# Which queue brings the first blocks of x and w1, and where TensorE's first run over w1 stands among x's turns

## The chip, the core and the metric

The kernel runs on one NeuronCore of a Trainium2 chip. The core has a matrix engine (TensorE, PE in the profile; its weight loads are PEld), VectorE (DVE), ScalarE (ACT), GpSimd (POOL) and a queue engine (SyncE, SP). Sixteen DMA engines move data between DRAM and the core's SBUF; transfers are issued here by SP and by ScalarE. Matmul results go to eight PSUM banks of 512 float32 columns. The metric is the device time of one execution in microseconds (us), taken as the median of several; smaller is better.

## The reference

The forward pass of a two-layer block with a tanh-approximated gelu, and its gradients. All inputs and outputs are bfloat16: x and grad_out are 2048 x 448, w1 is 448 x 1792, w2 is 1792 x 448.

```python
def _fwd_reference(x, w1, b1, w2, b2):
    h = jnp.einsum("bsd,df->bsf", x, w1) + b1
    h = _gelu(h)
    return jnp.einsum("bsf,fd->bsd", h, w2) + b2
# outputs: the result, and its gradients to x, w1, b1, w2, b2 for grad_out
```

## The kernel before

Rows of x (S = 2048) are worked in four blocks of 512; the 1792 hidden columns are 14 tiles of 128, taken as seven pairs. For each block and pair TensorE computes u = w1^T x^T (hidden columns on partitions, rows of x on the free axis), the other engines make gelu(u) and its derivative, and TensorE computes q = w2 grad_out^T and the products that use them. At the end come the gradients of w1 and w2, each a long sum over all rows. 448 is three times 128 plus 64, so a product over it is cut in halves of 64 contraction rows, and two halves run on TensorE at the same time in its upper and lower rows; in the profile one matmul "64*128 64x512" is one of two that run together, a pair.

Nothing is scheduled by a planner. Five tables of names, one for each engine (`PE_ORDER`, `ACT_ORDER`, `DVE_ORDER`, `SP_ORDER`, and a short list for GpSimd), give the order in which each engine's instructions are issued, and waits between engines follow from what each step reads and writes. An engine works through its list in order, so a step that waits holds back all behind it on that engine. DMAs signal their landing on eight semaphore slots (DMAHW0 to DMAHW7) in turn, in the order in which they are put into the program; the DMA that takes a slot for the second time waits on its queue until the first holder has landed.

The change touches the first ten microseconds. The names there are:

- On SP and ScalarE: `xr01`, `xr12`, `xr24` load rows 0 to 127, 128 to 255 and 256 to 511 of x (x's tiles 0, 1, and 2 and 3; function `LXN`, line 558 in the profile as for all plain loads) into `TR`. `L0` to `L4` load five parts of w1's first 384 rows into `w1f`; `L1` is in two pieces. `Z0` to `Z2` load its last rows, the left-over of 448 beyond 3 x 128, into `gh_nat`. `b1` is the first bias. `K0`, `K1` and so on load w2. `L1a` waits for the identity matrix.
- On VectorE: `ident` builds the identity (line 613 is its last step); `X0.0`, `X1.0`, `X2.1`, `X3.1` copy turned tiles of x from PSUM to SBUF (`XC`, line 633), and `b1T` copies the turned bias. ScalarE copies the other halves, after its table load (line 765).
- On TensorE: `W6` is six matmuls on constants, 128 x 512, that only wake the engine (`wake`, line 389). `X0` to `X3` turn x's four tiles against the identity (`XT`; eight matmuls of 64 columns each). `F6` is six pairs on constants, 128 columns wide (`fill`). `S0` is the first run over w1: pair 0, columns of x's tiles 0 and 1, all contraction rows at once in four banks (`U` with d = 3, `uq_run`). It issues second(0), second(1), then first(0) to first(3), then second(2); first(3) and second(2) read w1's left-over rows. `B` turns the bias. `T1` is pair 0 over x's tiles 2 and 3, one tile at a time. `u1.1`, `h1.2`, `u1.2`, `u2.1`, `u3.1` are further runs over w1: `u2.1` needs its third part (`L2`), `u3.1` the fourth (`L3`). `p0.0` is the first product that needs a gelu.
- All runs of halves are issued in the function `run`, so their matmuls share line 242. In lines 440, 442, 444 and 455 the first values of u get their bias.

The matmuls of S0 go to banks 4 to 7; the constants of W6 and F6 go to `qb`, that is banks 6 and 7, and are overwritten.

Of the kernel before, what the change touches and what calls it, by code (L numbers as in the profile page):

```python
# [88 lines left out]


PE_ORDER = """
W6 X0 X1 F6 X2 X3 S0 B T1 u1.1 h1.2 u1.2 u2.1 u3.1 u2.2 u3.2 p0.0 p0.1 p0.2 p0.3 p1.0 p1.1 p1.2 u4.1 u5.1 u4.2
u5.2 p1.3 p2.0 p2.1 p2.2 p2.3 u6.1 p3.0 u6.2 p3.1 p3.2 p3.3 p4.0 p4.1 u7.1 p4.2 u7.2 p4.3 p5.0 p5.1 p5.2 p5.3 u8.1
p6.0 u8.2 q0.1 p6.1 q0.2 u9.1 p6.2 u9.2 q1.1 p6.3 q1.2 u10.1 o1.0.0.6.1 u10.2 q2.1 o1.1.0.6.1 u11.1 q2.2 u11.2
o1.0.0.6.2 o1.1.0.6.2 q3.1 u12.1 q3.2 u12.2 o1.0.6.10.1 q4.1 o1.1.6.10.1 u13.1 q4.2 u13.2 o1.0.6.10.2 q5.1 o1.1.6.10.2
# [11 lines left out]
x3.1.6.10.1 x3.0.6.10.2 x3.1.6.10.2 x3.0.10.14.1 x3.1.10.14.1 x3.0.10.14.2 x3.1.10.14.2  # L107
"""
ACT_ORDER = """
xr12 L0 Z0 table X0.1 X1.1 X2.0 X3.0 k0A k0B c0A1 s0 g0 s1 g1 c2B t0 s2 g2 g3 s3 c5B g4 t1 t2 c6B g5 g6 s4 s5 g7 c8A c8B g8 c9A c9B  # L110
g9 c10A c10B t3 t4 g10 s6 c11A c11B s7 g11 t5 c12A c12B g12 s8 t6 c13A c13B g13 s9 t7 s10 t8 c14A c14B t9 g14 s11 s12
c15A c15B t10 g15 c16A c16B s13 t11 g16 c17A c17B s14 t12 g17 c18A c18B s15 g18 vx0.2 c19A c19B t13 t14 g19 s16 c20A
c20B s17 g20 t15 s18 t16 s19 c21A c21B t17 g21 c22A c22B s20 t18 g22 c23A c23B g23 s21 t19 s22 t20 s23 c24A c24B t21
# [12 lines left out]
vx3.3  # L126
"""
SP_ORDER = """
xr01 xr24 b1 L1a L1b Z1 L2 L3 K0 K1 L4 Z2 K2 K3 X1 R F b2 Y0 J0 J1 J2 Y1 I0 E J3 I1 So0.1 So0.0 X2 H0 H1 H2 H3 H4 H5 H6 H7 H8 H9
T0 T1 H10 T2 H11 T3 H12 T4 H13 T5 So1.0 So1.1 T6 T7 H14 T8 Y2 H15 T9 X3 H16 T10 H17 Sx0.0 Sx0.1 T11 H18 H19 T12 H20  # L130
T13 T14 T15 So2.0 Y3 H21 So2.1 T16 H22 H23 T17 T18 T19 H24 Sx1.0 T20 Sx1.1 H25 T21 H26 Nx H27 T22 T23 Sx2.0 Sx2.1 T24
T25 T26 So3.0 So3.1 Ng T27 Sx3.0 Sx3.1
# [28 lines left out]
def make_plan(tc, ctx, x, w1, b1, w2, b2, grad_out, out_0, out_1, out_2, out_3, out_4, out_5):  # L161
    nc = tc.nc
    P = 128
    _, S, D = x.shape
    F = w1.shape[1]
    NS, NF, SB = S // P, F // P, 512
# [7 lines left out]
    g2 = grad_out.rearrange("b s d -> (b s) d")  # L174
# [11 lines left out]
    w1_sb = w1f[:, 0:4 * F].rearrange("p (k f) -> p k f", k=4)  # L186
# [6 lines left out]
    xT = [sb.tile([P, 4, EDGE + SB], BF16, name=f"xT{i}") for i in range(2)]  # L193
# [23 lines left out]
    def bk_(i):  # L217
        return BK[i][:, :] if i < 6 else qb[:, i - 6, :]
# [8 lines left out]
    def run(slots, idle=False):  # L227


        first = slots[0]  # L230
        prev = [tail_of.get((first[i][0], 1 - i), (0, None, False)) for i in (0, 1)]
        prev = max([t for i, t in enumerate(prev) if t[2] or not first[i][4]], default=(0, None), key=lambda t: t[0])
        n_run[0] += 1
        word = None
        if prev[0] > seen[0]:
            word = nc.gpsimd.nop()  # L236
            tc.add_manual_dep(word.ins, prev[1].ins.name, DEP, reason="the run has ended")
            seen[0] = prev[0]
        for two in slots:
            for i, (b, n, l, r, st, sp) in enumerate(two):  # L240
                at, n = n if isinstance(n, tuple) else (0, n)
                m = nc.tensor.matmul(bk_(b)[:, at:at + n], lhsT=l, rhs=r, start=st, stop=sp, skip_group_check=True)  # L242
                if word is not None:
                    tc.add_manual_dep(m.ins, word.ins.name, DEP, reason="the halves change banks")
                    word = None
        for i in (0, 1):
            tail_of[slots[-1][i][0], i] = (n_run[0], m, idle)

    def uq_run(w, t, banks, pair, d, c0=0, c1=SB, at=0):

        ft = (2 * (pair % NPB), 2 * (pair % NPB) + 1)

        def plain(i, k, low, st, sp, banks=banks):
            rows = slice(0, 64) if low else slice(64, 128)
            cols = slice(ft[i] * P, (ft[i] + 1) * P)
            return (banks[i], (at, c1 - c0), w[rows, k, cols] if k < 3 else w1z[rows, cols], t[rows, k, EDGE + c0:EDGE + c1], st, sp)

        if w is w1_sb and pair < NPB and d < 3:
            if d == 1:
                run([(plain(1, k, True, k + at == 0, False), plain(0, k, False, k + at == 0, False)) for k in (0, 1, 2, 3)])
            else:
                run([(plain(0, k, True, False, k == 2), plain(1, (0, 1, 3)[k], False, False, k == 2)) for k in (0, 1, 2)])
            return

        if d == 3:
            one_, two = banks[:2], banks[2:]

            def first(k):
                return [plain(1, k, True, k == 0, k == 3, one_), plain(0, k, False, k == 0, k == 3, one_)]

            def second(k):
                return [plain(0, k, True, k == 0, k == 2, two), plain(1, (0, 1, 3)[k], False, k == 0, k == 2, two)]

            run([second(0), second(1)])
            run([first(k) for k in range(4)])
            run([second(2)])
            return  # L280
# [48 lines left out]
    def part_w1(p):  # L329
        return ("w1", W1_PART[p % NPB])  # L330

    def U(p, d, hf=None, by_tile=False):
        b = p // NPB
        if hf is None:
            bk, hs, c, tag = u_banks(p), (0, 1), (0, SB), ""
            vs = [bank(("u", p, 0), bk[0]), bank(("u", p, 1), bk[1])]
        else:
            bk, hs, c, tag = ((4, 5), (0, 1))[hf], (hf,), (256 * hf, 256 * hf + 256), f"h{hf}"
            vs = [bank(("u", p, 0, hf), bk[0]), bank(("u", p, 1, hf), bk[1])]
            if d == 3:  # L340
                bk = bk + (6, 7)
                vs += [bank(("ux", p, 0), 6), bank(("ux", p, 1), 7)]
        rd = [part_w1(p)] + [("xT", b, h) for h in hs] + ([("w1z", REST[p])] if b == 0 else ["w1r"])
        if d == 2 and b > 0:
            rd += [("xe", b), "w1f"]
        def fn():
            for a in range(c[0], c[1], P) if by_tile else (c[0],):
                uq_run(w1_sb, xT[b % 2], bk, p, d, a, a + P if by_tile else c[1], a - c[0])

        pe(f"u{p}.{d}{tag}", fn, rd, vs,  # L350
           ("s512" if hf is None else "s256", 2 + d), (bk, d))

    def Q(p, d):
# [169 lines left out]
    for i, t in enumerate([t for t in SP_ORDER.split() if t[0] == "S"]):  # L523
        b, half = t[2:].split(".")
# [166 lines left out]
    def num(t):  # L691
        return [int(i) for i in t.split(".")]

    for t in PE_ORDER.split():
        k, a = t[0], t[1:]
        if k == "w":
            wake(int(a), P)
        elif k == "W":
            wake(int(a))
        elif k == "X":  # L700
            XT(int(a))
        elif k == "f":
            fill(int(a), (3, 2), 2 * P)
        elif k == "F":
            fill(int(a), (6, 7), 2 * P)
        elif k == "B":
            pe("b1u", lambda: nc.tensor.matmul(bk_(5)[:, 256:272], lhsT=b1n[0:64, :], rhs=ident[0:64, 0:16], start=True, stop=True,  # L707
                                               skip_group_check=True), ["b1n", "b1z", "ident"], [val(("b1u",), ("bank5b",))], ("s16", 1), (None, 0))
        elif k == "d":
            DM(*num(a))  # L710
        elif k == "h":
            hf, d = num(a)
            U(0, d, hf)
        elif k == "S":
            U(0, 3, int(a))
        elif k == "T":
            U(0, 1, int(a), True)
        elif k in "uqp":
            {"u": U, "q": Q, "p": OP}[k](*num(a))
        else:  # L720
            b, half, f0, f1, d = num(a)
            UN(k, b, half, list(range(f0, f1)), d)
# [52 lines left out]
    for t in SP_ORDER.split():  # L775
        k, a = t[0], t[1:]
# [57 lines left out]
    for ft in range(NF):  # L834
        bk = next_bank()
# [8 lines left out]
        fn = (lambda dst=dst, src=src: nc.scalar.mul(out=dst, in_=src, mul=-0.5)) if eng == "ACT" else \  # L844
# [3 lines left out]
        c = ft // 4  # L848
# [37 lines left out]
    for ft in range(NF):  # L886
        halves = [(0, D)] if ft < NF - 1 else [(0, D - P), (D - P, D)]
        for (d0, d1) in halves:
            bk = next_bank()
# [8 lines left out]
            fn = (lambda dst=dst, src=src: nc.scalar.copy(out=dst, in_=src)) if eng == "ACT" else \  # L898
# [38 lines left out]
```

## Time and profile before

| What | Value |
|---|---|
| median of 3 runs | 263.88 us (263.86 to 264.1) |
| span of the profiled execution, first to last instruction | 262.2 us |
| TensorE busy | 258.8 us, 99% |
| VectorE busy | 199.5 us, 76% |
| ScalarE busy | 127.6 us, 49% |
| chain of waits that ended last | PE 99% |
| mean rate of all DMA | 178 GB/s |

The device time of a run contains what lies before the first and after the last instruction; the span does not. For the profiled execution only the span is told. A row of the timeline gives the start in us from the span's start, the length, the engine, the line, the operation, what is written and read, shapes and the count; neighbours of one form are merged. In brackets stands the idle time before it and what ended that. A matmul's length is longer than the distance to the next, since they are pipelined; the pace is read from the starts.

### The profile page before, as it was taken

Reading aid. Unit: us, or ns where it says so; the run is one execution under the profiler, and the core shown is the slowest. Engines: PE = TensorE matmul, PEld = TensorE weight load, DVE = VectorE, ACT = ScalarE, POOL = GpSimd, SP = SyncE. Lnnn points to the kernel's source line nnn. Section 1 sums busy time; section 2 is a strip of 40 time slices with the busy share of each in tenths; the row PEclk is TensorE's granted clock in tenths of the full one; section 3 lists DMA queues with packets and bytes.
Section 4 is the critical chain, followed back from the end, with each engine's and each line's share of the span. In section 5 each row is a group of like instructions: output and inputs, shape, how many; then the busy total and the mean of one; then the engine's idle time right before and its main releaser. Section 6 shows DMA issues by size and latency. Waiting matters only on the chain.

```text
span 262.2 us, 5415 instructions
## 1 busy us (share of the span) xinstructions
PE 258.8 (99%) x2217; PEld 149.5 (57%) x2217; DVE 199.5 (76%) x287; ACT 127.6 (49%) x166; POOL 14.2 (5%) x11
## 2 busy tenths in 40 slices
PE   8999999999999999999999999999999999999995
PEld 5444455555555666666666677765555555555554
DVE  5999398999989989999997995249999999310000
ACT  5899569936898956875896310011121111000001
POOL 1000000000000000000000000000000392400000
PEclk9999999999999999999999999999999999999999
DMA  6999989999999892972487824974899999975221
GB/s 201 292 249 171 197 127 197 258 341 212 244 180 220 236 228 43 195 203 43 107 203 257 216 42 63 262 211 106 162 217 136 184 213 171 235 152 158 72 70 35
DMA packets 120633, 46.61 MB, mean 178 GB/s; under 512 B 96686, under 2 KB 120479, under 8 KB 120608
## 3 DMA queue, kind: packets, MB, share of 16 engines
q1 hardware_dynamic: 119920, 45.82, 78.0%
q10 hardware_dynamic: 688, 0.44, 0.6%
q8 instruction: 17, 0.28, 0.4%
q14 instruction: 8, 0.07, 0.1%
HBM read 8.20 MB, written 14.28 MB: 86 GB/s over the span
## 4 chain that ended last, share of the span: by engine, by line
PE 99%; ACT 0%; issue 0%
PE bank L242 48%; PE qb L242 18%; PE bank L839 16%; PE bank L893 16%; PE qb L389 1%; ACT w_sb L898 0%; PE bank L707 0%
## 5 line engine op out<-in xcount | busy, mean ns | idle before, releaser
L242 PEld LDWEIGHTS <-HG 64*128 64x128 bf16 x896 | 55.7, 94 | 32.2 <-POOLq L236 2.1
L242 PE MATMUL qb<-gT,w2Tf 64*128 64x512 bf16 x392 | 52.9, 376 | 0.0
L242 PE MATMUL bank<-w_sb,HG 64*128 64x448 bf16 x448 | 48.4, 349 | 0.0
L242 PE MATMUL bank<-xT,w1f 64*128 64x512 bf16 (+2 forms) x361 | 47.3, 368 | 0.0
L242 PE MATMUL bank<-w1T_sb,HG 64*128 64x448 bf16 x448 | 47.2, 349 | 0.0
L515 DVE SCALAR_TENSOR_TENSOR HG<-TR,qb 128x1024 bf16<-128x1024 bf16 x28 | 34.1, 1217 | 12.6 <-PE qb L242 12.6
L893 PE MATMUL bank<-w2Tf,HG 128*128 128x448 bf16 (+2 forms) x240 | 42.6, 340 | 0.0
L839 PE MATMUL bank<-w1f,gh_nat 128*128 128x448 bf16 x224 | 42.5, 352 | 0.0
L893 PEld LDWEIGHTS <-HG 128*128 128x128 bf16 x240 | 22.9, 98 | 19.8
L839 PEld LDWEIGHTS <-gh_nat 128*128 128x128 bf16 x224 | 21.8, 98 | 20.6 <-issue 0.4
L242 PEld LDWEIGHTS <-w2Tf 64*128 64x128 bf16 x392 | 24.1, 94 | 16.6 <-POOLq L236 0.3
L500 ACT ACTIVATE TR<-TR 128x1024 bf16<-128x1024 bf16 x28 | 29.2, 1052 | 6.6 <-DVE TR L490 6.6
L242 PEld LDWEIGHTS <-w1f 64*128 64x128 bf16 x388 | 22.0, 94 | 17.3 <-POOLq L236 0.7
L862 DVE TENSOR_TENSOR w1T_sb<-w1T_sb,gh_nat 128x1792 f32<-128x1792 f32 x14 | 28.4, 2025 | 0.5
L844 ACT ACTIVATE TR<-bank 128x448 bf16<-128x448 f32 x14 | 7.6, 543 | 34.9 <-PE bank L839 34.9
L899 DVE CAST w_sb<-bank 128x448 bf16<-128x448 f32 x6 | 3.7, 624 | 25.9 <-PE bank L893 25.9
L898 ACT CAST w_sb<-bank 128x448 bf16<-128x448 f32 (+2 forms) x9 | 4.4, 490 | 37.7 <-PE bank L893 37.7
L868 POOL PARTITION_ALL_REDUCE w1T_sb<-w1T_sb x1 | 10.6, 10570 | 206.0 <-DVE w1T_sb L866 206.0
L475 ACT ACTIVATE TR<-gh_nat 128x1024 bf16<-128x1024 bf16 x15 | 15.7, 1052 | 11.5 <-DVE TR L510 11.5
L505 DVE TENSOR_SCALAR TR<-TR 128x2048 bf16<-128x2048 bf16 x28 | 19.2, 688 | 1.9 <-ACT TR L500 1.9
L495 DVE TENSOR_TENSOR TR<-TR,HG 128x1024 bf16<-128x1024 bf16 x28 | 19.2, 684 | 0.0
L510 DVE TENSOR_TENSOR TR<-TR 128x1024 bf16<-128x1024 bf16 x28 | 19.0, 686 | 0.1
(54 smaller groups left out, 190.6 us busy)
## 6 DMA issues: line engine op xcount, KB each, us to landing
hT_dram<-HG SPq DMA_DIRECT2D x28, 256.0 KB, 3.2
out_dram<-st SPq DMA_DIRECT2D x16, 224.0 KB, 3.3
w1f<-in_x_dram SPq DMA_DIRECT2D x2, 896.0 KB, 6.0
w2Tf<-in_grad_out_dram SPq DMA_DIRECT2D x1, 1792.0 KB
out_dram<-w_sb SPq DMA_DIRECT2D x2, 448.0 KB, 2.8
out_dram<-xT SPq DMA_DIRECT2D x2, 384.0 KB, 3.4
w_sb<-in_w_dram SPq DMA_DIRECT2D x1, 672.0 KB
w1f<-in_w_dram SPq DMA_DIRECT2D x1, 576.0 KB
```

The source lines that it names most:

```text
L242: m = nc.tensor.matmul(bk_(b)[:, at:at + n], lhsT=l, rhs=r, start=st, stop=sp, skip_group_check=True)
L475: pl.op("ACT", f"s{p}", lambda: nc.scalar.activation(out=TR[p % NTR][:, 1], in_=ubuf(p), func=ACT.Square, scale=sc), [("ub", p)], [v], ("a ...
L495: pl.op("DVE", f"R{p}", lambda: nc.vector.tensor_tensor(out=t[:, 1], in0=t[:, 1], in1=hblk(p), op=ALU.mult), [("r", p), ("h", p)], [val((" ...
L500: pl.op("ACT", f"t{p}", lambda: nc.scalar.activation(out=t[:, 0], in_=t[:, 0], func=ACT.Tanh), [("y", p)], [val(("t", p), ("TR0", p % NTR) ...
L505: pl.op("DVE", f"m{p}", lambda: nc.vector.tensor_scalar(out=t[:], in0=t[:], scalar1=1.0, scalar2=None, op0=ALU.subtract), [("t", p), ("r2" ...
L510: pl.op("DVE", f"n{p}", lambda: nc.vector.tensor_tensor(out=t[:, 0], in0=t[:, 0], in1=t[:, 1], op=ALU.mult), [("m0", p), ("m1", p)], [val( ...
L515: pl.op("DVE", f"G{p}", lambda: nc.vector.scalar_tensor_tensor(out=ghblk(p), in0=t[:, 0], scalar=2.0, in1=qb[:, :, :], op0=ALU.subtract, o ...
L839: nc.tensor.matmul(bk_(bk)[:, 0:D], lhsT=gh_nat[:, st // 4, ft, st % 4, :], rhs=x_nat[:, st, :], start=(st == 0), stop=(st == NS - 1))
L844: fn = (lambda dst=dst, src=src: nc.scalar.mul(out=dst, in_=src, mul=-0.5)) if eng == "ACT" else \
L862: nc.vector.tensor_tensor(out=hs3, in0=a, in1=gh_nat[:, st // 4, :, st % 4, :], op=ALU.add)
L868: pl.op("POOL", "gb1", lambda: nc.gpsimd.partition_all_reduce(gb1_w, hsum, channels=P, reduce_op=bass_isa.ReduceOp.add), ["hsc"], ["gb1"], ...
L893: nc.tensor.matmul(bk_(bk)[:, 0:d1 - d0], lhsT=h_nat[ft][:, st, :], rhs=g_nat[:, st, d0:d1], start=(st == 0), stop=(st == NS - 1))
```

## The change

ScalarE's queue no longer loads x's tile 1: its first two DMAs are now w1's first part and the left-over rows. SP loads tile 1 as its second DMA, ahead of tiles 2 and 3. On TensorE there is one waking matmul less (W5), two fill pairs now stand between X0 and X1 and five behind X1 (seven for six), and S0 is cut into four parts: S0.1 (second(0), second(1)) and S0.2 (first(0), first(1)) come ahead of X2 and X3, S0.3 (first(2), first(3)) and S0.4 (second(2)) behind them.

```diff
 PE_ORDER = """
-W6 X0 X1 F6 X2 X3 S0 B T1 u1.1 h1.2 u1.2 u2.1 u3.1 u2.2 u3.2 p0.0 ...
+W5 X0 F2 X1 F5 S0.1 S0.2 X2 X3 S0.3 S0.4 B T1 u1.1 h1.2 u1.2 u2.1 u3.1 u2.2 u3.2 p0.0 ...
...
 ACT_ORDER = """
-xr12 L0 Z0 table X0.1 X1.1 X2.0 X3.0 k0A k0B ...
+L0 Z0 table X0.1 X1.1 X2.0 X3.0 k0A k0B ...
...
 SP_ORDER = """
-xr01 xr24 b1 L1a L1b Z1 L2 L3 K0 K1 ...
+xr01 xr12 xr24 b1 L1a L1b Z1 L2 L3 K0 K1 ...
...
-            run([second(0), second(1)])
-            run([first(k) for k in range(4)])
-            run([second(2)])
+            run([[second(0), second(1)], [first(0), first(1)], [first(2), first(3)], [second(2)]][part - 1])
             return
```

On TensorE, at the place where the first run over w1 begins, stood before, behind X3's turns (`TR` is x, `st` the identity, `w1f` w1, `qb` and `bank` are PSUM, `xT` the turned x):

```order
99 L242 LDWEIGHTS TR_80
100 L242 MATMUL bank_92<-st_81,TR_80 128x64
101 L242 LDWEIGHTS w1f [waits DMAHW2_49]
102 L242 MATMUL qb<-xT_68,w1f 128x256
103 L242 LDWEIGHTS w1f
104 L242 MATMUL qb<-xT_68,w1f 128x256
```

Now the run's first matmul stands behind the fill, and waits for VectorE's and ScalarE's copies too; X2 stands behind the run's first eight matmuls, and the other six (four, then two) behind X3:

```order
69 L242 LDWEIGHTS const-bfloat16-1.0
70 L242 MATMUL qb<-const-bfloat16-1.0 128x128
71 L242 LDWEIGHTS w1f [waits DVE_49,DMAHW0_49]
72 L242 MATMUL qb<-xT_68,w1f 128x256 [waits Activation_49]
```

```order
85 L242 LDWEIGHTS w1f
86 L242 MATMUL bank_93<-xT_68,w1f 128x256
87 L242 LDWEIGHTS TR_80 [waits DMAHW4_49]
88 L242 MATMUL bank_89<-st_81,TR_80 128x64
```

Here X2 and X3 no longer wait for banks to be copied out, as the run between has waited for that already.

On SP, the first DMAs before:

```order
1 L558 DMA TR_80<-in_x_dram 128x448
2 L558 DMA TR_80<-in_x_dram 128x2x448
3 L558 DMA b1n<-in_b_dram 14x128 [waits Pool_49]
4 L558 DMA w1f<-in_w_dram 128x2x256 [waits DVE_49]
5 L558 DMA w1f<-in_w_dram 128x256
6 L558 DMA gh_nat<-in_w_dram 128x512 [waits DMAHW0_49]
7 L558 DMA w1f<-in_w_dram 128x3x256 [waits DMAHW1_49]
```

and now:

```order
1 L556 DMA TR_80<-in_x_dram 128x448 x2
2 L556 DMA TR_80<-in_x_dram 128x2x448
3 L556 DMA b1n<-in_b_dram 14x128 [waits Pool_49]
4 L556 DMA w1f<-in_w_dram 128x2x256 [waits DVE_49]
5 L556 DMA w1f<-in_w_dram 128x256
6 L556 DMA gh_nat<-in_w_dram 128x512 [waits DMAHW0_49]
7 L556 DMA w1f<-in_w_dram 128x3x256 [waits DMAHW1_49]
```

Row 1 now holds two loads, tiles 0 and 1. Row 6, `Z1`, still waits for slot 0; that slot was held by x's tile 1 on ScalarE's queue (X1 waited for it) and is now held by w1's first part (S0.1 waits for it).

More of the change, by code (lines that the diff above doesn't have):

```diff
@@ L91 @@
 PE_ORDER = """
-W6 X0 X1 F6 X2 X3 S0 B T1 u1.1 h1.2 u1.2 u2.1 u3.1 u2.2 u3.2 p0.0 p0.1 p0.2 p0.3 p1.0 p1.1 p1.2 u4.1 u5.1 u4.2
+W5 X0 F2 X1 F5 S0.1 S0.2 X2 X3 S0.3 S0.4 B T1 u1.1 h1.2 u1.2 u2.1 u3.1 u2.2 u3.2 p0.0 p0.1 p0.2 p0.3 p1.0 p1.1 p1.2 u4.1 u5.1 u4.2
 u5.2 p1.3 p2.0 p2.1 p2.2 p2.3 u6.1 p3.0 u6.2 p3.1 p3.2 p3.3 p4.0 p4.1 u7.1 p4.2 u7.2 p4.3 p5.0 p5.1 p5.2 p5.3 u8.1
@@ L109 @@
 ACT_ORDER = """
-xr12 L0 Z0 table X0.1 X1.1 X2.0 X3.0 k0A k0B c0A1 s0 g0 s1 g1 c2B t0 s2 g2 g3 s3 c5B g4 t1 t2 c6B g5 g6 s4 s5 g7 c8A c8B g8 c9A c9B
+L0 Z0 table X0.1 X1.1 X2.0 X3.0 k0A k0B c0A1 s0 g0 s1 g1 c2B t0 s2 g2 g3 s3 c5B g4 t1 t2 c6B g5 g6 s4 s5 g7 c8A c8B g8 c9A c9B
 g9 c10A c10B t3 t4 g10 s6 c11A c11B s7 g11 t5 c12A c12B g12 s8 t6 c13A c13B g13 s9 t7 s10 t8 c14A c14B t9 g14 s11 s12
@@ L128 @@
 SP_ORDER = """
-xr01 xr24 b1 L1a L1b Z1 L2 L3 K0 K1 L4 Z2 K2 K3 X1 R F b2 Y0 J0 J1 J2 Y1 I0 E J3 I1 So0.1 So0.0 X2 H0 H1 H2 H3 H4 H5 H6 H7 H8 H9
+xr01 xr12 xr24 b1 L1a L1b Z1 L2 L3 K0 K1 L4 Z2 K2 K3 X1 R F b2 Y0 J0 J1 J2 Y1 I0 E J3 I1 So0.1 So0.0 X2 H0 H1 H2 H3 H4 H5 H6 H7 H8 H9
 T0 T1 H10 T2 H11 T3 H12 T4 H13 T5 So1.0 So1.1 T6 T7 H14 T8 Y2 H15 T9 X3 H16 T10 H17 Sx0.0 Sx0.1 T11 H18 H19 T12 H20
@@ L247, in run, with uq_run @@
             tail_of[slots[-1][i][0], i] = (n_run[0], m, idle)
-    def uq_run(w, t, banks, pair, d, c0=0, c1=SB, at=0):
+    def uq_run(w, t, banks, pair, d, c0=0, c1=SB, at=0, part=0):
         ft = (2 * (pair % NPB), 2 * (pair % NPB) + 1)
@@ L330, in part_w1, with U @@
         return ("w1", W1_PART[p % NPB])
-    def U(p, d, hf=None, by_tile=False):
+    def U(p, d, hf=None, by_tile=False, part=0):
         b = p // NPB
@@ L347, in fn @@
             for a in range(c[0], c[1], P) if by_tile else (c[0],):
-                uq_run(w1_sb, xT[b % 2], bk, p, d, a, a + P if by_tile else c[1], a - c[0])
-        pe(f"u{p}.{d}{tag}", fn, rd, vs,
+                uq_run(w1_sb, xT[b % 2], bk, p, d, a, a + P if by_tile else c[1], a - c[0], part)
+        pe(f"u{p}.{d}{tag}.{part}", fn, rd, vs,
            ("s512" if hf is None else "s256", 2 + d), (bk, d))
@@ L714, in make_plan @@
         elif k == "S":
-            U(0, 3, int(a))
+            hf, part = num(a)
+            U(0, 3, hf, part=part)
         elif k == "T":
```

## Prediction

> **What bounds the kernel now.** I read the page first (busy shares, chain of waits), then a table of windows to see where TensorE (PE) ever stops, then the timeline of the first 10 us by engine, then the DMA issues of that stretch with their time to landing.
>
> ```profile
> PE 258.8 (99%) x2217; PEld 149.5 (57%) x2217; DVE 199.5 (76%) x287; ACT 127.6 (49%) x166; POOL 14.2 (5%) x11
> PE 99%; ACT 0%; issue 0%
> 9.01:258.00 248.99, 248.99 (x2089) 143.56 (x2090) 193.96 (x269) 121.96 (x155) 13.44 (x2) 1.00 0.80 179
> ```
>
> The second row is the chain of waits: PE carries it. The third is the windows view: from 9.01 to 258 us PE is busy 248.99 of 248.99 us. The work there is the same in both kernels, so the change reaches the end only by moving the moment at which this unbroken stretch begins, and that is u3.1, the first run over w1's fourth part. The start, in PE's timeline (start, length, group, count), with some rows taken from narrow windows so that groups are cut where I need them:
>
> ```profile
> 2.85 0.63 PE L389 MATMUL qb<-const-bfloat16-1.0 128*128 128x512 bf16 x1
> 3.41 0.61 PE L242 MATMUL bank<-st,TR 64*128 64x64 bf16 x16
> ...
> 3.62 0.40 PE L242 MATMUL bank<-st,TR 64*128 64x64 bf16 x8
> 3.83 0.83 PE L242 MATMUL qb<-const-bfloat16-1.0 64*128 64x128 bf16 x12
> 4.45 0.51 PE L242 MATMUL bank<-st,TR 64*128 64x64 bf16 x16
> 4.80 0.38 PE L242 MATMUL qb<-xT,w1f 64*128 64x256 bf16 x4
> 5.02 0.49 PE L242 MATMUL bank<-xT,w1f 64*128 64x256 bf16 x6
> ...
> 5.56 0.35 PE L242 MATMUL bank<-xT,w1f 64*128 64x128 bf16 x6
> ...
> 5.89 0.34 PE L242 MATMUL bank<-xT,w1f 64*128 64x128 bf16 x6
> ...
> 8.38 0.40 PE L242 MATMUL qb<-xT,w1f 64*128 64x512 bf16 x2
> 8.59 0.40 PE L242 MATMUL qb<-xT,gh_nat 64*128 64x512 bf16 x2
> 9.00 0.11 PEld L242 LDWEIGHTS <-w1f 64*128 64x128 bf16 x4 [0.51 <-DMA w1f<-in_w_dram]
> ```
>
> In order: the last of the six waking matmuls (2.85); X0 and X1, the turns of x's tiles 0 and 1 (3.41, 3.62); the fill F6 (3.83); X2 and X3 (4.45); S0 (4.80); T1's two tiles (5.56 and 5.89). The runs behind follow one another until u2.1's last pair at 8.59, a pair every 0.21, so PE is free at 8.80 and u3.1, at 9.01, has waited 0.2 us for a load of w1. There are two speeds: six fill pairs of 128 columns take 0.62 us (3.83 to 4.45), 0.10 each; two S0 pairs of 256 columns take 0.22 (4.80 to 5.02), 0.11 each. PE runs at half rate until about 4.65, although the granted clock reads 1.00 throughout.
>
> The other rows that count are VectorE's, which make the identity and copy x's turns to SBUF (ScalarE copies the other half, faster), and the loads:
>
> ```profile
> 2.63 0.25 DVE L613 TENSOR_SCALAR st<-st 128x128 bf16<-128x128 bf16 x1
> 3.84 0.76 DVE L633 CAST xT<-bank 128x256 bf16<-128x256 f32 x2 [0.96 <-PE bank L242]
> 4.98 0.76 DVE L633 CAST xT<-bank 128x256 bf16<-128x256 f32 x2 [0.39 <-PE bank L242]
> 3.50 0.21 ACT L765 ACTIVATE tiny<-const-bfloat16-1.0 128x1 bf16<-128x1 bf16 x1
> 0.72 0.87 SPq L558 DMA_DIRECT2D TR<-in_x_dram  x2
> 1.63 0.50 SPq L558 DMA_DIRECT2D b1n<-in_b_dram  x1
> 1.15 0.47 ACTq L558 DMA_DIRECT2D w1f<-in_w_dram  x1
> 3.87 0.43 SPq L558 DMA_DIRECT2D gh_nat<-in_w_dram  x1
> 4.34 0.98 SPq L558 DMA_DIRECT2D w1f<-in_w_dram  x2
> ```
> ```profile
> TR<-in_x_dram SPq DMA_DIRECT2D x1, 112.0 KB, 2.5
> TR<-in_x_dram SPq DMA_DIRECT2D x1, 224.0 KB, 3.1
> w1f<-in_w_dram ACTq DMA_DIRECT2D x1, 192.0 KB, 3.5
> w1f<-in_w_dram SPq DMA_DIRECT2D x1, 128.0 KB, 2.7
> w1f<-in_w_dram SPq DMA_DIRECT2D x1, 192.0 KB, 4.1
> ```
>
> The last figure is issue to landing. x's tile 0 lands at 0.72 + 2.5 = 3.2, and X0 follows at 3.41. Tiles 2 and 3, issued about 1.16, land at about 4.25. w1's first part, 1.15 + 3.5, lands at 4.65, just ahead of S0. Its fourth part, issued halfway through the last SP row (4.83), lands at 8.95: u3.1's wait.
>
> **The change part by part.** *Loads.* ScalarE's queue loses tile 1, so w1's first part is issued at 0.72 instead of 1.15. SP issues tile 1 second, tiles 2 and 3 third, at about 1.63 where b1 stood: 0.47 later. b1 goes to about 2.1, still before L1a, which waits for the identity (2.63 + 0.25 = 2.88), so SP's later issues are not pushed by that. Tile 0 now competes with w1's 512-byte rows instead of tile 1's whole rows. I take it to land 0.3 to 0.4 earlier, since in the first 0.8 us the engines served two x loads at once; the bounds are the old 3.2 and 2.85, with which the identity takes over.
>
> ```profile
> 1.70:2.50 0.80, 0.80 (x4) 0.25 (x3) 0.62 (x3) 0.29 (x1) 0.00 (x0) 1.00 0.84 216
> 3.30:4.65 1.35, 1.35 (x37) 1.24 (x37) 0.76 (x2) 1.04 (x4) 0.00 (x0) 1.00 1.08 332
> ```
>
> In the windows view DMA is the share before last: 1.08 in 3.3 to 4.65, so the engines are full and what w1 gains there x's later tiles lose. For tiles 2 and 3 I keep the 3.1: 1.63 + 3.1 = 4.73, bounds 4.25 and 1.63 + 3.5 = 5.13. The Trainium skill, "DMA: Bandwidth & Descriptors", section "Issuing engines are not separate DMA queues", says the same of queues in general: all issuers share the same engines, and spreading saves only issue time. By it the move could gain at most the order among the loads; the 1.08 agrees.
>
> *PE, X0.* W5 in place of W6 frees PE at 2.85 instead of 3.27. X0 starts between 2.98 (identity plus 0.1) and 3.41 (nothing gained). I take 3.05. The removed waking matmul lay wholly in the wait for tile 0, and the one added fill pair (2 + 5 for 6) lies in waits too: nothing.
>
> *PE, S0's first half.* X0 takes 0.21 at half rate, F2 0.21, so X1 starts at X0 + 0.42 and its products are complete 0.40 later (row 3.62). Before, VectorE's two copies overlapped and took 0.76; now the second starts behind the later X1 and takes a bit over half, 0.42. T1's second tile starts 0.15 behind its last copy (4.98 + 0.76 = 5.74 to 5.89); with that, S0.1 starts at X0 + 0.42 + 0.40 + 0.03 + 0.42 + 0.15 = X0 + 1.42 = 4.47. w1's first part must have landed: 0.72 + 2.7 = 3.4 to 0.72 + 3.5 = 4.2, so it no longer decides. F5 ends at X1 + 0.21 + 0.52 = 4.20, so PE waits 0.27. S0.1 and S0.2 are four pairs: one before 4.65 at 0.21 and three at 0.11, 0.54 in all. So X2 starts at 5.01 (0.44 at full rate, 0.84 at half). Tiles 2 and 3, landed at 4.73, do not hold it; at the bound 5.13 they would, by 0.2.
>
> *PE, x's last turns.* Here the cost sits. X2 and X3 stood at 4.45 and stand at 5.01. Before, T1's second tile came 1.44 behind X2's start (5.89), held by the copies; X2 and X3 took 0.35 then and take about 0.24 at full rate, so 1.33 now: 6.34. Before, the whole of S0 (4.80 to 5.56, 0.76) covered these copies. Now only S0.3 and S0.4 do (three pairs, 0.33), and PE stands for some 0.4 us. The bias product B and the copy of b1 behind it, and with them ScalarE's and VectorE's first steps, move by the same amount. What waits for those is p0.0, for the first gelu:
>
> ```profile
> 9.07 1.04 ACT L470 ACTIVATE HG<-ub 128x1024 bf16<-128x1024 bf16 x1
> ...
> 11.17 2.81 PE L242 MATMUL bank<-w_sb,HG 64*128 64x448 bf16 x28
> ```
>
> The gelu ends at 10.11, p0.0 starts at 11.17: 1.06 of room, so 0.45 costs nothing there.
>
> *Sum.* T1's second tile from 5.89 to 6.34: 0.45 later. The runs up to u2.1 follow unbroken, so PE is free at 8.80 + 0.45 = 9.25; u3.1 at 9.25 instead of 9.01, since 0.2 of it falls into the old wait: +0.24 us. The profiled execution has a span of 262.2 us, 1.7 below the median of 263.88, which I take for what lies around every span; so 262.4 for the span, **264.1 us** for the time, +0.1%.
>
> *Bounds.* X0 at 2.98, S0.1 at 4.40 and the full rate from there: X2 at 4.84, T1's second tile 6.17, u3.1 at 9.08, +0.07. X0 at 3.41: S0.1 at 4.83, X2 at 5.27, T1 6.60, u3.1 9.51, +0.5.
>
> *SP's semaphores.* The load of w1's left-over rows on SP (3.87) waits for slot 0; that was tile 1 on ScalarE's queue and is now w1's first part, landing between 3.4 and 4.2. It and all SP issues behind it move by 0 to 0.35, u3.1's load from 8.95 to at most 9.30. I take 0.1: 9.05, below 9.25, so it costs nothing. The next loads from DRAM come after u3.1 and move alike.
>
> **Rivals.** *The copies are hidden after all (263.7 to 263.9).* If x's last tiles land at 4.25 and the copies of tile 1 end early enough that X2 starts by 4.55, T1 is where it was; and if u3.1's load then comes early too, the old 0.2 wait goes: 263.88 - 0.2 = 263.7. For it: the table load ends 0.4 earlier (3.50 was the last step before the copies), so ScalarE's copies are never late. Against: S0.1 cannot start before X0 + 1.42, so 4.40 + 0.44 = 4.84 even at the best.
>
> *Tile 0 comes no earlier (264.4).* w1's 192 KB take as much of the engines as tile 1's 112 KB did: X0 at 3.41, the bound +0.5. For it: the 0.84 share in 1.70 to 2.50. Against: tile 0 is then alone in front of SP's queue.
>
> *u3.1's load comes later (264.2 to 264.4).* Slot 0 clears at 4.2, u3.1's load lands at 9.30, u3.1 at 9.35: +0.35. It decides from a delay of 0.3 us.
>
> *The full rate comes late (265.7, slower).* PE stands longer (0.27 before S0.1, 0.4 before T1) and has one waking matmul less; if what sets the rate sees too little work, it stays at half. From 4.65 to, say, 8.55 (the same 3.9 us again that it took from the first matmul at 0.76) half of the work is lost: 1.95, of which the wait ahead of T1 takes 0.4 in: 1.55 beside the 0.24, so 265.7. It decides past 0.2% when the rate changes 1.4 us later (0.7 lost, 0.4 taken in, 0.24). Against: up to 4.65 PE's work is nearly what it was. The Trainium skill, "TensorE: Matmul & The Clock Gate", section "What's actually happening", has a rule for this: the array is throttled until a free-running window of some 3.4 us was busy. The 3.9 us here fit. By the rule a later change costs a whole window.
>
> **How the numbers follow.** The sum, with its own range 263.95 to 264.4 (the bounds; tile 0 no earlier is its upper end): 0.62, of that tile 0 no earlier 0.15. Hidden: 0.20. u3.1's load late: 0.08. Late full rate: 0.07. Something faster than these: 0.03. The range from 263.6 to 264.75 takes in the hidden case and its 0.1 of scatter, and above 264.4 the sums of two delays; it leaves out the late clock. 0.2%, which a measurement of this kernel can just tell, is 0.53 us: faster 0.04 (PE would have to reach u3.1 by 8.48), slower 0.12 (the late clock, and two delays added), the same 0.84.
>
> **What would show it.** Right: X0 near 3.05, X2 at about 5.0, a gap ahead of T1 and its second tile near 6.3, w1's first part landing ahead of 4.3, and u3.1 at 9.2 to 9.3 with no wait for a load. Wrong: T1 at or before 5.9; pairs of 256 columns still 0.21 apart after 5 us; or PE gaps after u3.1, which would mean that ScalarE's and VectorE's chains have less room than I think.

## The result, and the profile after

The changed kernel takes 266.3 us (median of six, 264.79 to 266.47) where the kernel before takes 264.01 (median of six, 263.86 to 264.33): a ratio of 1.0068, 95% interval 1.0054 to 1.0082. It is slower by 0.68%, and the forecast of 264.1 with no change was wrong; 266.3 lies above the range. The two medians lie 2.29 us apart, 0.87%, the two means 0.72%: the six executions of the changed kernel lie 1.7 us apart, two of them well below the rest (264.79 and 265.4), those of the kernel before 0.5. In the runs below, three single executions took 343 to 346 us at a granted clock of 0.76, and they are in no range and in no count here.

The page of the changed kernel, busy shares and chain of waits:

```profile
PE 260.6 (98%) x2218; PEld 149.2 (56%) x2218; DVE 199.6 (75%) x287; ACT 127.8 (48%) x166; POOL 14.2 (5%) x11
PE 97%; DMA 1%; SPq 0%; ACT 0%; issue 0%
```

PE is busy 1.8 us longer with one matmul more (2218 for 2217): the same work ran slower. A transfer, 1%, is now on the chain. The windows view from u3.1 on:

```profile
11.41:260.40 248.99, 248.99 (x2091) 142.31 (x2088) 194.18 (x270) 122.22 (x155) 13.44 (x2) 1.00 0.79 176
```

It is the stretch of 248.99 us that began at 9.01 before, unbroken as before. From the start of u3.1 to the end of the span lie 262.2 - 9.01 = 253.2 us before and 264.6 - 11.41 = 253.2 now. The profiled execution took 266.39 us, 1.8 more than its span of 264.6. So all that was lost, 2.40 us in the profile, was lost ahead of u3.1. PE's timeline there (start, length, group, count, and in brackets the idle time before it):

```profile
3.27 0.40 PE L242 MATMUL bank<-st,TR 64*128 64x64 bf16 x8 [0.22 <-DMA TR<-in_x_dram]
3.48 0.40 PE L242 MATMUL qb<-const-bfloat16-1.0 64*128 64x128 bf16 x4
4.21 0.40 PE L242 MATMUL bank<-st,TR 64*128 64x64 bf16 x8 [0.32 <-DMA TR<-in_x_dram]
4.41 0.72 PE L242 MATMUL qb<-const-bfloat16-1.0 64*128 64x128 bf16 x10
5.20 0.61 PE L242 MATMUL qb<-xT,w1f 64*128 64x256 bf16 x4
5.58 0.66 PE L242 MATMUL bank<-xT,w1f 64*128 64x256 bf16 x4
6.01 0.66 PE L242 MATMUL bank<-st,TR 64*128 64x64 bf16 x16
6.45 0.43 PE L242 MATMUL bank<-xT,w1f 64*128 64x256 bf16 x2
...
7.53 0.53 PE L242 MATMUL bank<-xT,w1f 64*128 64x128 bf16 x6
7.95 1.49 PE L242 MATMUL bank<-xT,w1f 64*128 64x512 bf16 x6
9.23 0.51 PE L242 MATMUL bank<-xT,gh_nat 64*128 64x512 bf16 x2
9.57 0.49 PE L242 MATMUL bank<-xT,w1f 64*128 64x256 bf16 x5
```

Two things stand in it. First, X1 (4.21) waits for x's tile 1, which is only now behind tile 0 on SP's queue; before, X1 followed X0 without a wait. Second, the half rate lasts: S0.1's and S0.2's four pairs of 256 columns take 5.20 to 6.01, 0.20 each, where two pairs took 0.22 before; three pairs of 512 columns take 7.95 to 9.23, 0.43 each. Only from about 9.4 on is the pace full; before, it was full from 4.65 on. The granted clock in the windows reads 1.00 in both kernels at both paces, so the pace has to be taken from the starts.

The loads of x's tile 1 and of its tiles 2 and 3, from issue to landing (SP issued them at 1.16 and 1.63):

```profile
TR<-in_x_dram SPq DMA_DIRECT2D x1, 112.0 KB, 3.0
TR<-in_x_dram SPq DMA_DIRECT2D x1, 224.0 KB, 3.5
```

Tile 1 landed at 4.16; before, it landed at 3.42 on ScalarE's queue. Tiles 2 and 3 landed at 5.16 (4.23 before). w1's first part landed at 3.85 (4.70), and u3.1's load at 8.23 (8.96), so that nothing waits for it any more. The view prints no landing for tile 1 before and for w1's first part now; for these two the time is that of the last of the sixteen signals on their semaphore slot in the trace.

A second series gave the same, and its profile another moment for the full rate:

> The changed kernel once more, for a second profile of the same program. If the moment of the full rate is set by the instructions alone, it comes at 9.4 again, with u3.1 at 11.4. If it runs on a beat of its own, it comes at another moment between 5.5 and 9.4, u3.1 between 9.8 and 11.4, and the time follows as 253.2 plus u3.1 plus 1.8; tile 1 lands at 4.0 to 4.2 in either case. Times again between 264.8 and 266.5.

It took 266.05 us (265.74 to 266.72), 1.008 of the kernel before (1.0056 to 1.0105). PE's timeline in it:

```profile
8.03 1.25 PE L242 MATMUL bank<-xT,w1f 64*128 64x512 bf16 x6
9.12 0.38 PE L242 MATMUL bank<-xT,gh_nat 64*128 64x512 bf16 x2
9.34 0.49 PE L242 MATMUL bank<-xT,w1f 64*128 64x256 bf16 x5
```

The first pairs are 0.43 apart and the last is 0.22 long (9.12 to 9.34), so the rate changes at about 8.9, within the row of six, half a microsecond sooner than in the first profile. u3.1 is at 11.18.

### The profile page after: what moved, and what is told of

Read it like the earlier page. It is cut to its first block, busy times and chain, and to the rows that moved or that the text cites. A ratio compares the mean times of both kernels' runs of the same rounds, so it can differ in the third digit from the quotient of the medians.

```text
span 264.6 us, 5418 instructions
## 1 busy us (share of the span) xinstructions
PE 260.6 (98%) x2218; PEld 149.2 (56%) x2218; DVE 199.6 (75%) x287; ACT 127.8 (48%) x166; POOL 14.2 (5%) x11
## 4 chain that ended last, share of the span: by engine, by line
PE 97%; DMA 1%; SPq 0%; ACT 0%; issue 0%
PE bank L242 48%; PE qb L242 18%; PE bank L838 16%; PE bank L892 16%; DMA TR<-in_x_dram 1%; SPq L556 0%; ACT w_sb L897 0%
## 5 line engine op out<-in xcount | busy, mean ns | idle before, releaser
L242 PEld LDWEIGHTS <-HG 64*128 64x128 bf16 x896 | 55.0, 94 | 32.9 <-POOLq L236 2.1
L242 PE MATMUL bank<-xT,w1f 64*128 64x512 bf16 (+2 forms) x361 | 48.8, 377 | 0.0
```

## The experiments

My theory after this profile: PE stands idle too much in its first microseconds, keeps its half rate for 4 to 5 us longer, and this costs most. Its rivals: the waits for x's tiles cost by themselves (late loads), or the new order does (the copies of x's last tiles have too little cover).

### Idle time without any other change

The order and the loads of the kernel before, but one waking matmul and the fill taken out:

```diff
-W6 X0 X1 F6 X2 X3 S0 B T1 ...
+W5 X0 X1 X2 X3 S0 B T1 ...
```

> The kernel before with one waking matmul less and without the six fill pairs ahead of X2 (W5 X0 X1 X2 X3 S0); no load is moved. PE then stands idle about 1.1 us more before S0 (0.43 ahead of X0, 0.6 ahead of X2), and no step of real work can start later. Theory of the late rate (idle time before S0 keeps PE at half rate for longer, and that is most of the 2.4 us lost): 264.8 to 266.5 us, matmuls of 256 columns still 0.21 us apart in S0. Theory of the late data (x's tile 1 landing at 4.16 us is the cause): 263.9 to 264.1, no change.

Measured: 265.48 us (264.9 to 265.99), 1.0052 (1.0034 to 1.0069) of the 264.05 that the kernel before took beside it. PE's timeline:

```profile
3.32 0.61 PE L242 MATMUL bank<-st,TR 64*128 64x64 bf16 x16 [0.27 <-DMA TR<-in_x_dram]
4.37 0.61 PE L242 MATMUL bank<-st,TR 64*128 64x64 bf16 x16 [0.44 <-DMA TR<-in_x_dram]
4.79 0.62 PE L242 MATMUL qb<-xT,w1f 64*128 64x256 bf16 x4
5.19 0.85 PE L242 MATMUL bank<-xT,w1f 64*128 64x256 bf16 x6
...
7.12 1.51 PE L242 MATMUL bank<-xT,w1f 64*128 64x512 bf16 x6
8.40 0.65 PE L242 MATMUL bank<-xT,gh_nat 64*128 64x512 bf16 x2
8.82 0.65 PE L242 MATMUL bank<-xT,w1f 64*128 64x256 bf16 x4
```

S0 starts at 4.79, where it started before (4.80): the work taken out was constants only, and nothing that follows came later for it. Yet its pairs are 0.2 apart (4.79 to 5.19), pairs of 512 columns 0.43 (7.12 to 8.40), and u3.1 starts at 10.97 instead of 9.01. Matmuls that compute nothing were worth 1.4 us in the median.

### The changed kernel with its idle time filled

```diff
-W5 X0 F2 X1 F5 S0.1 S0.2 X2 X3 S0.3 S0.4 B T1 ...
+W6 X0 F7 X1 F8 S0.1 S0.2 X2 X3 S0.3 S0.4 B T1 ...
```

> The changed kernel with more matmuls on constants, so that PE does not stand still (W6 X0 F7 X1 F8 S0.1): the loads stay late, the idle time of 1.2 us ahead of S0.1 goes. Late rate: full rate from 4.6 to 6 us on, S0.1 at 5.2, X2 at 5.65, T1's second tile at 7.0, u3.1 at 9.9, time 264.6 to 265.2. Late data: still 266.0 to 266.5, since the same data come at the same time.

Measured: 265.03 us (264.67 to 265.64), 1.0035 (1.0023 to 1.0046). The loads are as late as in the changed kernel. PE's timeline:

```profile
3.41 0.40 PE L242 MATMUL bank<-st,TR 64*128 64x64 bf16 x8
3.62 0.65 PE L242 MATMUL qb<-const-bfloat16-1.0 64*128 64x128 bf16 x14
4.11 0.28 PE L242 MATMUL bank<-st,TR 64*128 64x64 bf16 x8
4.22 0.63 PE L242 MATMUL qb<-const-bfloat16-1.0 64*128 64x128 bf16 x16
4.99 0.40 PE L242 MATMUL qb<-xT,w1f 64*128 64x256 bf16 x4
5.21 0.40 PE L242 MATMUL bank<-xT,w1f 64*128 64x256 bf16 x4
5.43 0.41 PE L242 MATMUL bank<-st,TR 64*128 64x64 bf16 x16
...
6.33 0.34 PE L242 MATMUL bank<-xT,w1f 64*128 64x128 bf16 x6 [0.16 <-DVE xT L631]
...
6.75 0.34 PE L242 MATMUL bank<-xT,w1f 64*128 64x128 bf16 x6
```

The seven fill pairs take 0.49 (3.62 to 4.11) and the rate changes within them, at 3.8. S0.1 to X2 takes 0.44 (4.99 to 5.43) instead of 0.81, and u3.1 starts at 9.67 instead of 11.41. That is 1.27 us of the median's 2.25 back (266.3 - 265.03, and 266.3 - 264.05). In the profile 0.66 us is left (9.67 against 9.01), with the rate full from 3.8 on: that part is not the rate. The medians leave about 1 us; the profiled execution is the fastest of the ten, so some of the rest may be a later full rate in the others, of which there is no profile. T1's second tile stands 1.32 behind X2 (5.43 to 6.75), and the wait for VectorE's copies is in the first of the two T1 rows.

### Twice the idle time

```diff
-W6 X0 X1 F6 X2 X3 S0 B T1 ...
+W1 X0 X1 X2 X3 S0 B T1 ...
```

> The kernel before with one waking matmul of six and no fill pairs (W1 X0 X1 X2 X3 S0): 2.2 us of standstill ahead of X0 and 0.6 ahead of X2, twice and more the idle time of the run with W5 and no fill; no step of real work can start later. Late rate: 265.5 to 266.8, the full rate later than 7 us. If idle time ahead of X0 does not count and only that behind it does: as with W5 and no fill, 265.0 to 265.6.

Measured: 265.56 us (264.62 to 266.29), 1.0042 (1.0026 to 1.0059). PE stands for 1.98 us ahead of X0 in the timeline, and the full rate comes at about 7.95:

```profile
3.32 0.61 PE L242 MATMUL bank<-st,TR 64*128 64x64 bf16 x16 [1.98 <-DMA TR<-in_x_dram]
...
7.10 1.23 PE L242 MATMUL bank<-xT,w1f 64*128 64x512 bf16 x6
8.17 0.38 PE L242 MATMUL bank<-xT,gh_nat 64*128 64x512 bf16 x2
```

More than twice the idle time costs no more than the 265.48 of the first experiment, and with one waking matmul for five the full rate came sooner (7.95 for 9.4). So the rate isn't earned matmul by matmul. It fits a stretch of time that has been too idle, behind which one stretch more passes at half rate; how much of it an execution pays varies (264.62 to 266.29). The value lies in the ranges of both theories, so this run doesn't tell whether idle time ahead of X0 counts as the rest does.

### One waking matmul less, alone

```diff
-W6 X0 X1 F6 X2 X3 S0 B T1 ...
+W5 X0 X1 F6 X2 X3 S0 B T1 ...
```

> The kernel before with one waking matmul less, and nothing else: 0.43 us more of idle time ahead of X0, no work can start later. Late rate with idle time counted anywhere: some executions change rate later, median 264.2 to 265.0. If only a long standstill counts, or if idle time is harmless: 263.9 to 264.2.

Measured: 264.12 us, 1.0008 (0.9989 to 1.0027) of 263.91. Nine of its ten executions lie between 263.79 and 264.69, one took 266.47, which is the changed kernel's time. Whether W5 alone loses the rate now and then can't be told from one such execution. Usually it doesn't.

### The two halves of the change, each alone

Only the loads of the change, in PE's old order:

```diff
-xr12 L0 Z0 table X0.1 ...
+L0 Z0 table X0.1 ...
...
-xr01 xr24 b1 L1a ...
+xr01 xr12 xr24 b1 L1a ...
```

> Only the loads are moved, PE's order is that of before (W6 X0 X1 F6 X2 X3 S0). X1 should wait for tile 1 until 4.2, X2 for tiles 2 and 3 until 5.3. Late rate: PE idles 0.7 us ahead of X1 and 0.2 ahead of X2, the full rate comes late in some executions or all: 265 to 266.5. Late data alone: S0 at 5.6 for 4.80, +0.8 less the old wait of 0.2 ahead of u3.1: 264.6 to 264.8. If the loads are harmless and PE's new order is at fault: 263.9 to 264.1.

Measured: 264.42 us, 1.0027 (1.0002 to 1.0052); seven of nine executions from 264.26 to 264.44, two at 266.14 and 266.77. PE's timeline of the profiled one (264.42):

```profile
4.15 0.39 PE L242 MATMUL bank<-st,TR 64*128 64x64 bf16 x8 [0.35 <-DMA TR<-in_x_dram]
4.36 0.71 PE L242 MATMUL qb<-const-bfloat16-1.0 64*128 64x128 bf16 x12
5.18 0.41 PE L242 MATMUL bank<-st,TR 64*128 64x64 bf16 x16
5.42 0.38 PE L242 MATMUL qb<-xT,w1f 64*128 64x256 bf16 x4
```

X1 waits for tile 1 here too, and S0 starts at 5.42 instead of 4.80, because all four tiles must be turned ahead of it; u3.1 starts at 9.43, +0.42. The rate changes at about 4.8, within the fill: its pairs start 0.11 apart up to 4.77, and the next follows after 0.09.

Only PE's new order, with the old loads:

```diff
-W6 X0 X1 F6 X2 X3 S0 B T1 ...
+W5 X0 F2 X1 F5 S0.1 S0.2 X2 X3 S0.3 S0.4 B T1 ...
```

> Only PE's order is changed (W5 X0 F2 X1 F5 S0.1 S0.2 X2 X3 S0.3 S0.4), the loads stand as before. X0 at 3.4 with 0.45 idle ahead of it, X1 at 3.83, S0.1 at 4.8, X2 at 5.25, T1's second tile at 6.6. Late rate: less idle time (0.6 us) than in the changed kernel, so full rate at about 5 in most executions: 264.3 to 264.7, and more if 0.6 us of idle time is already too much. Late data: no load is late, so at most the 0.5 us of the later copies, 264.4.

Measured: 265.02 us (264.34 to 265.43), 1.0029 (1.0017 to 1.0042). X1 starts at 3.68, without a wait for tile 1, but S0.1 still waits for w1's first part and starts at 4.95; the full rate comes at about 7.1, and u3.1 at 10.16. Behind X0 this profile and that of the loads alone have the same idle time ahead of the change of rate (0.52 and 0.53); ahead of X0 they differ (0.43 and 0.14), and only here the rate came late. That suggests that idle time ahead of X0 counts too, from one profile each.

The same with the idle time filled, to have the order's own price at full rate:

```diff
-W5 X0 F2 X1 F5 S0.1 S0.2 X2 X3 S0.3 S0.4 B T1 ...
+W6 X0 F2 X1 F8 S0.1 S0.2 X2 X3 S0.3 S0.4 B T1 ...
```

> PE's new order with the loads as before, and PE kept busy with constants (W6 X0 F2 X1 F8 S0.1 S0.2 X2 X3 S0.3 S0.4): neither late data nor idle time ahead of S0.1, so what is left is the cost of the order itself, x's last copies with only half of S0 over them. If that costs: full rate from 4 to 5.5, S0.1 at 4.8 to 4.9 with w1's first part, X2 at 5.3, T1's second tile at 6.6, u3.1 at 9.5, 264.3 to 264.7. If the order costs nothing once the rate is right: 263.8 to 264.1.

Measured: 264.86 us (264.41 to 265.11), 1.0024 (1.001 to 1.0038). PE's timeline:

```profile
4.83 0.39 PE L242 MATMUL qb<-xT,w1f 64*128 64x256 bf16 x4
5.05 0.40 PE L242 MATMUL bank<-xT,w1f 64*128 64x256 bf16 x4
5.27 0.41 PE L242 MATMUL bank<-st,TR 64*128 64x64 bf16 x16
...
6.17 0.34 PE L242 MATMUL bank<-xT,w1f 64*128 64x128 bf16 x6 [0.16 <-DVE xT L631]
6.59 0.34 PE L242 MATMUL bank<-xT,w1f 64*128 64x128 bf16 x6
```

S0.1 starts at 4.83, close to where S0 started before (4.80), and the rate is full from 4.55. T1's second tile comes 1.32 behind X2, as the prediction had it, and it comes at 6.59 instead of 5.89: +0.70, of which the old wait of 0.2 at u3.1 takes its part (u3.1 at 9.51, +0.50). So the order costs 0.5 in a profile at full rate, and 0.75 in the medians taken side by side (264.86 against 264.11). The profiled execution (264.51) is one of the fastest of the ten, so the 0.75 may hold a later full rate in others.

### Where tile 1's delay comes from

ScalarE's two loads exchanged, so that w1's left-over rows (128 rows of 1,024 bytes) and not w1's first part (384 of 512) go out beside tile 0:

```diff
-L0 Z0 table X0.1 ...
+Z0 L0 table X0.1 ...
```

> The changed kernel with ScalarE's two loads in the other order: the left-over rows (128 pieces of 1024 bytes) first, w1's first part (384 pieces of 512 bytes) second. Theory A (x's tile 1 is late because it stands second in SP's queue): it still lands at 4.0 to 4.2, time 266. Theory B (it is late because the many pieces of w1's first part are made up for the DMA engines at the same time as x's): it lands at 3.3 to 3.7, w1's first part at 4.3 to 4.7, PE idles 0.5 us less, time 264.6 to 265.6.

Measured: 265.05 us (264.8 to 265.31), 1.0034 (1.0022 to 1.0045). Tile 1's load, the second on SP's queue (issued at 1.17), and that of w1's first part:

```profile
TR<-in_x_dram SPq DMA_DIRECT2D x1, 112.0 KB, 2.6
w1f<-in_w_dram ACTq DMA_DIRECT2D x1, 192.0 KB, 3.3
```

Tile 1 lands at 3.79, between the ranges of the two theories, and X1 starts at 3.84 without a wait; w1's first part, now issued second, lands at 4.43, in time for S0.1 at 4.85. X2 has to wait for tiles 2 and 3, which land at 5.50. This is about 1 us better than the changed kernel (266.3 and 266.05 in its two series). Its profile has the full rate by 4.85; it shows the fastest of nine executions, so the others may have had it later. With the constants put back in as well (W6, F3, F8):

```diff
-W5 X0 F2 X1 F5 S0.1 ...
+W6 X0 F3 X1 F8 S0.1 ...
```

> The changed kernel with the left-over rows ahead of w1's first part in ScalarE's queue, and PE kept busy with constants (W6 X0 F3 X1 F8 S0.1): against the changed kernel with fills, tile 1 lands 0.3 to 0.4 sooner and w1's first part at 4.4. If late data have a price of their own at the full rate: S0.1 at 4.85, u3.1 at 9.4 to 9.5, 264.4 to 264.7, that is 0.2 to 0.5 below the 265.0 of the changed kernel with fills. If they cost only through the rate: 265.0.

Measured: 264.70 us (264.59 to 265.21), 1.0022 (1.001 to 1.0035). It has the lowest median of all kernels with the new order, within their scatter, and is still slower than the kernel before. But the earlier data that it was to test did not come: tile 1 landed at 4.03, where it landed at 4.04 in the changed kernel with fills, and S0.1 starts at 4.97 (4.99) and u3.1 at 9.64 (9.67). So the 3.79 did not come again beside the same 128 rows, and this run doesn't price late data.

An attempt to let w1's first part go out later, behind ScalarE's table load, missed what it was made for:

```diff
-L0 Z0 table X0.1 ...
+table L0 Z0 X0.1 ...
```

> The changed kernel with both of ScalarE's loads behind its table load, so that they are issued from 2.0 on and x's first two tiles have the queues to themselves. Theory A: tile 1 still lands at 4.0 to 4.2. Theory B: tile 0 lands at 2.8 to 3.0 and tile 1 at 3.2 to 3.5. The time says little, as w1's first part lands only at 5 to 5.5 and holds S0.1: 265 to 267.

One execution, 265.31 us. ScalarE's timeline:

```profile
0.72 1.28 ACT L764 ACT_TABLE_LOAD   x1 [0.72 <-PEq L920]
0.78 0.43 ACTq L556 DMA_DIRECT2D w1f<-in_w_dram  x1
```

The table load runs from 0.72 to 2.00 and the DMA behind it is issued at 0.78 all the same, only 0.06 later than in the changed kernel. So this was the changed kernel once more: tile 1 landed at 4.06 and the full rate came at 6.9.

### A try at a faster kernel

If u3.1's wait of 0.2 us is all that the kernel before has left there, loading w1 sooner on SP should bring it in:

```diff
-xr01 xr24 b1 L1a L1b Z1 L2 L3 K0 ...
+xr01 xr24 b1 L1a L1b L2 L3 Z1 K0 ...
```

> The kernel before with SP issuing w1's third and fourth part ahead of the left-over rows (L2 L3 Z1 for Z1 L2 L3): u3.1's load is issued 0.44 us sooner. If the 0.2 us ahead of u3.1 is a wait for that load: it lands at 8.2 to 8.6, u3.1 at 8.8, time 263.7 to 263.9 (0.1 to 0.2 us gained). If the load is held up by one slow DMA engine wherever it stands: no change.

Measured: 263.89 us, 0.9994 (0.998 to 1.0008): no difference. u3.1's load lands at 7.74 and u3.1 starts at 8.88, free of it, 0.13 sooner. PE's timeline shows something else:

```profile
3.81 0.51 PE L242 MATMUL qb<-const-bfloat16-1.0 64*128 64x128 bf16 x12
4.63 0.41 PE L242 MATMUL bank<-st,TR 64*128 64x64 bf16 x16 [0.31 <-DVE xT L633]
```

F6 took 0.83 in the profile of before, from 3.83. Here, with the same list on PE, it takes 0.51: the full rate is there from about 3.8. X2 then waits 0.31 for the copies of the first tiles, and S0 starts only at 4.91, behind the landing of w1's first part (4.86), so that nothing of this is gained. The moment at which the rate changes differs from one execution to the next by nearly a microsecond with the same list on PE.

### Idle time and full rate, all in one table

The idle time ahead of the first run over w1 is worked out from the starts: the waking matmuls end at 3.27 (W6), 2.85 (W5) or 1.19 (W1), a turn takes 0.21 at half rate and a fill pair 0.10; what is left between the starts is idle. Where the full rate comes ahead of that run, only the idle time up to the change is counted. For the left-over rows first, the change falls into the wait of 0.28 ahead of S0.1, which is counted whole.

| Kernel | idle before the first run over w1 | full rate from | u3.1 | span of that profile |
|---|---|---|---|---|
| before | 0.14 | 4.65 | 9.01 | 262.2 |
| w1's later parts sooner | 0.14 | 3.8 | 8.88 | 262.1 |
| PE's order alone, filled | 0.14 | 4.55 | 9.51 | 262.7 |
| changed, filled | 0.14 | 3.8 | 9.67 | 262.9 |
| left-over rows first, filled | 0.14 | 3.6 | 9.64 | 262.9 |
| W5 alone | 0.49 | 4.85 | 8.79 | 262.0 |
| loads alone | 0.67 | 4.8 | 9.43 | 262.6 |
| left-over rows first | 0.86 | by 4.85 | 9.79 | 263.0 |
| PE's order alone | 0.97 | 7.1 | 10.16 | 263.4 |
| before with idle time | 1.10 | 9.4 | 10.97 | 264.2 |
| table load first | 1.10 | 6.9 | 10.29 | 263.5 |
| changed | 1.23 | 9.4 | 11.41 | 264.6 |
| changed, second profile | 1.29 | 8.9 | 11.18 | 264.4 |
| before with twice the idle time | 2.71 | 7.95 | 10.22 | 263.4 |

In every kernel the span minus u3.1 is 253.2, give or take 0.1. Up to 0.86 us of idle time the full rate came by 4.9 in the profiled executions, from 0.97 on it came between 6.9 and 9.4.

## Why the prediction was wrong, point by point

**What was right.** The end follows u3.1 by a fixed 253.2 us. The step "x's last turns" put T1's second tile 1.33 behind X2; 1.31 to 1.33 was measured wherever the new order ran at full rate. w1's first part landed ahead of 4.3 (3.85), SP's semaphores delayed nothing (the load on SP is still issued at 3.87), and PE is unbroken behind u3.1, so ScalarE's and VectorE's chains have the room. From S0.1 to u3.1 I had 9.25 - 4.47 = 4.78 us; at full rate it took 9.67 - 4.99 = 4.68.

**A miss that cost nothing.** Tiles 2 and 3 came later than the 4.73 of the sum and past its bound of 5.13: they landed at 5.16. X2 did not wait for them only because it started as late as 6.01.

**The step "S0's first half" was too short by 0.73 us.** It has X1 at "X0 + 0.42" and asks of the loads only when tile 0, w1's first part and tiles 2 and 3 land. Tile 1 was itself moved, from first in ScalarE's queue to second in SP's, and its landing never entered the sum. X0 came at 3.27 instead of 3.05, as tile 0 landed at 3.23 and gained nothing (this was a rival, at 0.15, which had X0 at 3.41); X1 came at 4.21 instead of 3.47, of which 0.52 is its own wait for tile 1; S0.1 came 0.99 behind X1 where I had 1.00. So S0.1 started at 5.20 and not at 4.47. The rows quoted in the prediction would have said it: SP's second DMA is issued at 1.16, a load of x takes 2.5 to 3.1, so 3.7 to 4.3 against the 3.47 that the sum used. Of the delay of 0.74 in its landing (3.42 to 4.16), 0.44 is the later issue and 0.3 a longer flight. The Trainium skill, "DMA: Bandwidth & Descriptors", section "Issuing engines are not separate DMA queues", which the prediction cited, grants to a second issuer only the time that issuing takes; that is the 0.44, and this kernel had been using it.

**Putting the constants at "nothing" was wrong, and the rival that contradicted it was given too small a chance.** I costed the removed waking matmul and the fill at nothing because their time fell into waits. Their time does; their effect is the rate. The late full rate had a chance of 0.07, with the argument that "up to 4.65 PE's work is nearly what it was". But the sum's own rows had a wait of 0.27 ahead of S0.1 and a waking matmul of 0.43 less, and with tile 1's wait it became 1.23 us of idle time against 0.14. The size of that rival was right: 1.55 us net of the waits that it takes in, where 6.21 - 4.68 = 1.53 was measured (S0.1 to u3.1 in the changed kernel, and with the idle time filled). That the two agree to 0.02 is luck: the second profile of the changed kernel has 11.18 - 5.29 = 5.89 there, and so 1.21. Its 265.7 fell short because it stood on a sum that was itself short.

**The sum, mended.** 0.24 forecast, plus 0.73 for S0.1's start, less 0.10 for the stretch to u3.1, plus 1.53 for the rate: 2.40, the whole difference of the two profiles. By experiment, filling takes 1.74 of the 2.40 away (11.41 to 9.67); of the 0.66 that stays, 0.50 is the order (9.51 with the old loads) and 0.16 the late loads. In the medians filling brings back 1.27 of 2.25, and the other 0.98 is the order (0.75 with the old loads) and the late loads, which add 0.2 to that (265.03 against 264.86) and lie within the scatter; some of the 0.98 may still be a later rate.

**What decides the rate.** All runs agree with a stretch that has to be busy enough: idle time alone brings the late rate, filling takes it away, more idle time costs no more. The Trainium skill, "TensorE: Matmul & The Clock Gate", section "What's actually happening", describes a free-running window of some 3.4 us that must be busy before the throttle goes. By it a failed window costs one window, and the moment depends on where the window lay when the kernel began. The traces agree that the moment shifts: the same list of PE gave 4.65 and 3.8, the changed kernel 9.4 and 8.9. They don't show the window itself, as the granted clock reads 1.00 at both paces. That a late rate is one failed window is an estimate, and it fits all fourteen profiles: lay that length back from the measured change, and the stretch that ended there held at most 0.81 us without a matmul, the time ahead of the first one included (0.16 before, 0.67 with the loads alone, 0.81 with the table load first); lay it back once more in the six profiles with a late rate, and that stretch held 0.87 (PE's order alone) to 2.72, and 1.23 in the changed kernel. How much idle time a window forgives is not shown more closely than that. By this it is partly luck on which side an execution falls, and the times agree, though no profile shows it: as the span behind u3.1 is fixed, the 264.79 of the changed kernel puts its u3.1 at about 9.8, so it had the full rate early, while an execution of W5 alone and two of the loads alone took more than 266. Why tile 1's flight was 0.3 longer isn't settled. Beside the 128 rows of the left-over part it landed at 3.79 once and at 4.03 once, beside w1's first part between 4.04 and 4.24, so neither theory of it is shown; the order of pieces inside the queues was not measured.

## What to carry to other kernels

Where TensorE is the bound from its first microseconds on, add up its idle time ahead of the first full-rate work in the new order, not only the stalls on the path: constants that fill a wait may be what brings the rate, and about 1 us of idle time cost 1.4 us here with nothing else moved. When a load is moved to another queue, write down the landing of that load first, from its new issue time and the nearest row, before asking what its removal does for the others. And read the pace from the distance between the starts of equal matmuls, since the column of the granted clock may show no difference.

## What was not expected of the hardware

- The rate isn't lost in proportion: 1.10 us of idle time cost 1.4 us (265.48 against 264.05), 2.71 us cost 1.45 (265.56 against 264.11).
- The half rate can last to 9.4 us, with PE almost unbroken busy from 5.2 on, and the moment moves by 0.5 to 0.9 us between two executions of one list on PE.
- A load that is the second on its queue landed 0.74 us later than as the first on another one, though it was issued only 0.44 later (3.42 and 4.16, in one profile each).
- ScalarE issues a DMA at 0.78 while its table load runs from 0.72 to 2.00: in that one execution a table load ahead of a DMA didn't hold it back.
